# A constant operand for the clock warm-up, an own buffer for the second row tile, and its load on ScalarE's queue

## The chip, the cores and the metric

The kernel runs on one core of one Trainium2 chip. The metric is the device time of one execution in microseconds (us), lower is better. "The trace" is the hardware profile of one execution, and its times count from the start of the span. The span is about 1.7 us shorter than the device time (193.2 against 194.91 us in the profiled run of before).

## The reference

A LayerNorm without gain feeds two branches, and both are added to the input: sliding-window attention (32 heads of 16, 8 keys at distance 2) and a gated GELU feed-forward network.

```python
# x: [1, 2048, 512] bf16; wqkv [512, 1536], wo [512, 512]; w_gate, w_up [512, 1376], w_down [1376, 512]
xn = _layernorm(x, axis=-1)                       # eps 1e-5
return x + _A_ref(xn, A_wqkv, A_wo) + _B_ref(xn, B_w_gate, B_w_up, B_w_down)
# _B_ref: (gelu(xn @ w_gate) * (xn @ w_up)) @ w_down
```

## The kernel before

The program builds a graph of tasks with priorities, and a scheduler in the source lays them out on the five engines. The 2048 rows are 16 tiles of 128. Only the first tiles matter here: until tile 0 is loaded, normalized and transposed, TensorE has no real work. It runs warm-up matmuls meanwhile, which are meant to bring its clock up: in the trace of before, the step to full speed comes 5.6 us after the first of them.

```python
# warm-up: VectorE clears wsrc, TensorE multiplies it with itself
G.task("dve", "c_wsrc", 0.25, lambda e: e.memset(wsrc[:, :], 0.0), wr=[I_wsrc], prio=PC - 1)
WARM = cfg.get("WARM", ([512] * 8 + [128], [512, 128]))    # before / after the first transposes
...     # per entry: matmul(PS[...], lhsT=wsrc[:, 0:128], rhs=wsrc[:, 0:wn]), rd=[I_wsrc]

# loads: all on SyncE's queue; tile 0, tile 1, first weights (q), tile 2, weights k, tile 3, weights v, ...
t_x = G.task("sp", "ld_x%d_%d" % (p, t2), 0, mk_ld(), wr=[(it_x, t2)],
             prio=((-960, -959), (-957.8, -956.5))[p][t2], nbytes=128 * 1024)

# tile 0: VectorE (bn_stats, bn_aggr); square root on ScalarE. Tile 1: statistics on ScalarE:
#   sx1 (sum) -> negm1 (-mean) -> sxx1 (sum of squares) -> var1 (divide) -> sq1 (square root)
# then on VectorE, in place: sub (x - mean), rstd (reciprocal), norm (times rstd)

# the order that the author fixed on each engine
chain(["bnst0", "bnag0", "sub0", "rstd0", "norm0", "mean1", "sub1", "evy0_0", "rstd1", "norm1",
       "evy0_1", "bnst2", ...])                                                        # VectorE
chain(["sx1", "sq0", "negm1", "sxx1", "var1", "sq1", "evx0_0", "evx0_1", "evq0_0", "sq2"])  # ScalarE
chain(warm_tasks[:len(WARM[0])] + ["tpx0_0"] + warm_tasks[len(WARM[0]):] +
      ["mma0_0", "tpx0_1", "mmt0_0", "mmt0_1", "mmt1_0", "tpx1_0", ...])               # TensorE

# the end of SyncE's program: before the last store, wait for all earlier transfers
if eng_name == "sp" and t is self.order["sp"][-1]:
    late = self.order["sp"][-5:]
    for (s, tot) in self.dma_totals:
        if not any(q.sem is s for q in late):
            e.wait_ge(s, tot)
...
for q in self.order["sp"][-5:]:      # after the last store
    e.wait_ge(q.sem, q.val)
```

Names used below: the *first transposes* are tpx0_0 (tile 0), the *first projection* is mma0_0 (eight matmuls of 128 columns on tile 0), and *tile 1's projections* begin with mmt0_1.

## Time and profile before

| | |
|---|---|
| device time, median of 3 | 194.56 us (194.54 to 194.84) |
| the profiled execution | 194.91 us |
| TensorE busy | 97% of the span |
| first warm-up matmul, first transposes, first projection | 1.51, 5.04, 6.23 us |
| clock step to full speed | 7.1 us |

The clock is read from the matmuls too: before the step, the warm-up matmuls of 512 columns start 0.427 us apart and matmuls of 128 columns 0.107; after it, those of 128 columns start 0.056 us apart. "Cold" and "slow" below mean the first pace, "warm" the second.

The prediction below shows the engines, the chain and the timeline. Here are the lines that it only tells. First two lines of the page: the span, and SyncE's transfer queue (packets, MB, share of 16 engines' span).

```profile
span 193.2 us, 3285 instructions
...
q1 hardware_dynamic: 34784, 26.83, 57.0%
```

From the timeline (start, length, engine, line, what): SyncE issues both row tiles, then the first weights.

```profile
0.80 0.88 SPq L927 DMA_DIRECT2D XIN<-in_A_x_dram  x2
...
1.72 0.43 SPq L879 DMA_DIRECT2D Wqkv<-in_A_wqkv_dram  x1
```

From the view of source line 563 (count, duration in ns, first and last start): the ten semaphore waits before the last store; by the trace's records they start about 0.06 us apart, from 190.65 to 191.20.

```profile
L563 SPq EVENT_SEMAPHORE  x10: 17/28/28, 190.6 to 191.2; - x10
```

One queue carries nearly everything, and the first issues take 0.4 to 0.5 us each. The waits run from 190.6 to 191.2 us while VectorE finishes the last block at 191.08, so they end after the data is ready.

### The profile page before, as it was taken

Reading aid. Unit: us, or ns where it says so; the run is one execution under the profiler, and the core shown is the slowest. Engines: PE = TensorE matmul, PEld = TensorE weight load, DVE = VectorE, ACT = ScalarE, POOL = GpSimd, SP = SyncE. Lnnn points to the kernel's source line nnn. Section 1 sums busy time; section 2 is a strip of 40 time slices with the busy share of each in tenths; the row PEclk is TensorE's granted clock in tenths of the full one; section 3 lists DMA queues with packets and bytes.
Section 4 is the critical chain, followed back from the end, with each engine's and each line's share of the span. In section 5 each row is a group of like instructions: output and inputs, shape, how many; then the busy total and the mean of one; then the engine's idle time right before and its main releaser. Section 6 shows DMA issues by size and latency. Waiting matters only on the chain.

```text
span 193.2 us, 3285 instructions
## 1 busy us (share of the span) xinstructions
PE 187.6 (97%) x1239; PEld 92.6 (48%) x1256; DVE 152.4 (79%) x240; ACT 106.1 (55%) x177; POOL 15.7 (8%) x31
## 2 busy tenths in 40 slices
PE   6999999999999999999999999999999999999994
PEld 2794444444444444444444444444444444444484
DVE  5699999999997975999995599998996099912132
ACT  5677565786897666703376677328276720058000
POOL 6010011110931020000000000000000000000000
PEclk9999999999999999999999999999999999999999
DMA  5999997899564014975500597420250497130121
GB/s 142 352 397 327 313 171 136 215 244 226 150 128 102 3 33 132 242 144 150 151 25 27 127 243 166 117 90 0 68 132 21 112 230 163 41 112 0 48 76 44
DMA packets 34801, 27.04 MB, mean 140 GB/s; under 512 B 11265, under 2 KB 33249, under 8 KB 34785
## 3 DMA queue, kind: packets, MB, share of 16 engines
q1 hardware_dynamic: 34784, 26.83, 57.0%
q8 instruction: 10, 0.16, 0.4%
q14 instruction: 7, 0.05, 0.1%
HBM read 19.99 MB, written 5.26 MB: 131 GB/s over the span
## 4 chain that ended last, share of the span: by engine, by line
PE 97%; issue 1%; DVE 0%; DVEq 0%
PE PS L1399 36%; PE PS L1478 20%; PE PS L1156 18%; PE PS L1474 7%; PE PS L1102 4%; PE PS L1367 4%; PE PS L1240 4%; PE PS L870 2%; PE PS L1434 2%; PE PS L1233 1%; PE PS L1044 1%; DVE OB L1498 0%; DVE wsrc L819 0%; DVE Wd L843 0%; DVEq L558 0%
## 5 line engine op out<-in xcount | busy, mean ns | idle before, releaser
L1416 ACT ACTIVATE UU<-PS 128x512 bf16<-128x512 f32 x40 | 24.1, 603 | 35.7 <-PE PS L1399 35.7
L1478 PE MATMUL PS<-Wd,HT 128*128 128x512 bf16 (+2 forms) x207 | 41.1, 345 | 0.1
L1399 PE MATMUL PS<-xnT,Wu 128*128 128x512 bf16 x155 | 39.8, 379 | 0.7 <-issue 0.5
L1399 PE MATMUL PS<-xnT,Wg 128*128 128x512 bf16 x155 | 39.2, 379 | 0.5 <-ACT OT L1379 0.2
L1210 DVE TENSOR_TENSOR UNI<-QT,KT 128x2048 bf16<-128x2048 bf16 x32 | 37.0, 1219 | 2.6 <-PE PS L1367 2.5
L1156 PE MATMUL PS<-xnT,Wqkv 128*128 128x512 bf16 x156 | 35.3, 379 | 0.2
L1421 DVE TENSOR_TENSOR HT<-GG,UU 128x512 bf16<-128x512 bf16 x40 | 16.6, 419 | 20.2 <-ACT UU L1416 20.1
L1409 ACT ACTIVATE GG<-PS 128x512 bf16<-128x512 f32 x40 | 23.7, 601 | 15.0 <-PE PS L1399 12.2
L1478 PEld LDWEIGHTS PS<-Wd,HT 128*128 128x128 bf16 x209 | 19.6, 98 | 18.6
L1399 PEld LDWEIGHTS PS<-xnT,Wu 128*128 128x128 bf16 x160 | 15.3, 98 | 19.6 <-issue 1.3
L1399 PEld LDWEIGHTS PS<-xnT,Wg 128*128 128x128 bf16 x160 | 15.5, 98 | 19.3 <-ACT OT L1379 0.4
L1156 PEld LDWEIGHTS PS<-xnT,Wqkv 128*128 128x128 bf16 x160 | 15.6, 98 | 18.6
L1347 DVE TENSOR_TENSOR BS<-BS,PT 128x2048 bf16<-128x2048 bf16 x16 | 19.6, 1223 | 0.4
L1347 DVE TENSOR_TENSOR UNI<-BS,PT 128x2048 bf16<-128x2048 bf16 x16 | 19.5, 1218 | 0.0
L1498 DVE TENSOR_TENSOR OB<-PS,XR 128x512 bf16<-128x512 f32 (+2 forms) x19 | 11.2, 604 | 10.0 <-PE PS L1478 9.9
L1474 PE MATMUL PS<-Wo,OT 128*128 128x512 bf16 (+2 forms) x76 | 16.9, 345 | 0.0
L1180 ACT ACTIVATE VT<-PS 128x512 bf16<-128x512 f32 x16 | 9.6, 597 | 4.4 <-PE PS L1156 4.4
L1379 ACT ACTIVATE OT<-PS 128x512 bf16<-128x512 f32 x16 | 8.3, 602 | 5.0 <-PE PS L1367 5.0
L944 DVE BATCH_NORM_STATS2 st<-XIN 128x6 f32<-128x512 bf16 x15 | 10.1, 686 | 0.9 <-DMA XIN<-in_A_x_dram 0.9
L1474 PEld LDWEIGHTS PS<-Wo,OT 128*128 128x128 bf16 x76 | 7.2, 98 | 7.0
L1196 POOL COPY KT<-KT 128x64 bf16<-128x64 bf16 x3 | 8.0, 2657 | 17.5 <-ACT KT L1173 16.1
L1166 ACT ACTIVATE QT<-PS 128x512 bf16<-128x512 f32 x12 | 7.2, 597 | 3.1 <-PE PS L1156 3.1
(73 smaller groups left out, 153.6 us busy)
## 6 DMA issues: line engine op xcount, KB each, us to landing
BS<-vt_scratch SPq DMA_DIRECT2D x64, 128.5 KB, 3.7
vt_scratch<-VT SPq DMA_DIRECT2D x16, 128.0 KB
XR<-in_A_x_dram SPq DMA_DIRECT2D x16, 128.0 KB, 2.3
out_dram<-OB SPq DMA_DIRECT2D x14, 128.0 KB, 1.8
Wqkv<-in_A_wqkv_dram SPq DMA_DIRECT2D x3, 512.0 KB
XIN<-in_A_x_dram SPq DMA_DIRECT2D x6, 256.0 KB, 4.5
Wg<-in_B_w_gate_dram SPq DMA_DIRECT2D x1, 1280.0 KB
Wu<-in_B_w_up_dram SPq DMA_DIRECT2D x1, 1280.0 KB
```

The costliest lines, as they stand in the source:

```text
L944: return lambda e: e.bn_stats(out=st[:, t, :], in_=XIN[:, it.slot, t2, :])
L1156: ins = e.matmul(PS[:, 512 * it.slot:512 * it.slot + HWD], lhsT=lhsT, rhs=xnT[:, itx.slot, kt, c0:c0 + HWD], start=(kt == 0), stop=(kt == 3))
L1180: return lambda e: e.activation(out=VT[:, ito.slot, 0:HWD], in_=PS[:, 512 * it.slot:512 * it.slot + HWD], func=ACTF.Identity)
L1210: return lambda e: e.tensor_tensor(out=UNI[:, it.slot, :, :], in0=bass.AP(QT, (itq.slot * 4 + g) * 512, [[NQT * 4 * 512, 128], [0, 4], [1, ...
L1347: return lambda e: e.tensor_tensor(out=dst(), in0=bass.AP(BS, it.slot * 4 * 514 + o, [[NBS * 4 * 514, 128], [514, 4], [128, 4], [1, 128]]) ...
L1399: ins = e.matmul(PS[0:M, 512 * it.slot:512 * it.slot + 512], lhsT=Wx[:, kt, j * 128:j * 128 + M], rhs=xnT[:, itx.slot, kt, :], start=(kt = ...
L1409: return lambda e: e.activation(out=GG[0:M, ito.slot, :], in_=PS[0:M, 512 * it.slot:512 * it.slot + 512], func=ACTF.Gelu_apprx_tanh)
L1416: return lambda e: e.activation(out=UU[0:M, ito.slot, :], in_=PS[0:M, 512 * it.slot:512 * it.slot + 512], func=ACTF.Identity)
L1421: return lambda e: e.tensor_tensor(out=HT[0:M, ito.slot, j, :], in0=GG[0:M, ig.slot, :], in1=UU[0:M, iu.slot, :], op=ALU.mult)
L1474: ins = e.matmul(PS[:, 512 * it.slot:512 * it.slot + CW], lhsT=OT[:, ito.slot, dq, ti * 128:(ti + 1) * 128], rhs=Wo[:, dq, c0:c1], start=( ...
L1478: ins = e.matmul(PS[:, 512 * it.slot:512 * it.slot + CW], lhsT=HT[:, ith.slot, j, ti * 128:(ti + 1) * 128], rhs=Wd[:, j, c0:c1], start=Fal ...
L1498: return lambda e: e.tensor_tensor(out=OB[:, ito.slot, 0:CW], in0=PS[:, 512 * it.slot:512 * it.slot + CW], in1=XR[:, itx.slot, c0:c1], op= ...
```

## The change

Its intent is to shorten the start and the end, the only places where TensorE isn't working. Warm-up matmuls read a constant that GpSimd writes at 0.36 us, before the other engines start at about 0.8, so TensorE can begin at once. Tile 1's load is issued by ScalarE at the same moment as tile 0's on SyncE. Tile 1 is centred into its own buffer XS, so VectorE need not wait until ScalarE has read the tile; and the division by 512 moves into the square root's scale, so var1 goes. The waits at the end move three stores ahead.

```diff
-            if eng_name == "sp" and t is self.order["sp"][-1]:
-                late = self.order["sp"][-5:]
+            if eng_name == "sp" and t is self.order["sp"][-4]:
+                late = self.order["sp"][-7:]
...
-            for q in self.order["sp"][-5:]:
+            for q in self.order["sp"][-7:]:
...
-        wsrc = sb("wsrc", [128, 512], BF)
+        one_l = nc.const_aps.tensor(1.0, [128, 128], BF)
+        one_r = nc.const_aps.tensor(1.0, [128, 512], BF)
...
+        XS = sb("XS", [128, 512], BF)
...
-        WARM = cfg.get("WARM", ([512] * 8 + [128], [512, 128]))
+        WARM = cfg.get("WARM", ([512] * 9 + [128], [512, 128, 128, 128, 128]))
...
+                    t_x.on_act = p == 0 and t2 == 1
...
-                            ("var1", 0.2, dict(out=mv[:, 1, 1:2], in_=sums[:, 2:3], ...
+                        return lambda e: e.activation(out=sq[:, 1:2], in_=sums[:, 2:3], func=ACTF.Sqrt,
+                                                      scale=1.0 / D, bias=eps[:, 0:1])
...
+                if t == 1:
+                            out=XS[:, :], in0=XIN[:, it.slot, 1, :], scalar1=mv[:, 1, 0:1], scalar2=None,
...             # norm1 reads XS instead of XIN; the rest renames, drops an unused option, and follows from this
```

More of the change, by code (lines that the diff above doesn't have):

```diff
@@ L674, in bass_parallel_sum__sliding_local_dilated__glu_gated_geglu__prompt_kernel @@
     NXIN = cfg.get("NXIN", 4)
-    NSUBA = cfg.get("NSUBA", 0)
     NSQA = cfg.get("NSQA", 4)
@@ L800, in bass_parallel_sum__sliding_local_dilated__glu_gated_geglu__prompt_kernel @@
         I_zpad = Item("zpad")
-        I_wsrc = Item("wsrc")
         I_onef = Item("onef")
@@ L809, in bass_parallel_sum__sliding_local_dilated__glu_gated_geglu__prompt_kernel @@
         I_sums = Item("sums")
+        I_xs = Item("XS")
         I_junk = Item("junk")
@@ L818, in bass_parallel_sum__sliding_local_dilated__glu_gated_geglu__prompt_kernel @@
         PC2 = cfg.get("PC2", 8)
-        G.task("dve", "c_wsrc", 0.25, lambda e: e.memset(wsrc[:, :], 0.0), wr=[I_wsrc], prio=PC - 1)
         G.task("pool", "c_ones", 0.2, lambda e: e.memset(cf[:, :], 1.0), wr=[I_cf], prio=PC)
@@ L869, in mk_w @@
             def mk_w(it=it_warm, wn=wn):
-                return lambda e: e.matmul(PS[:, 512 * it.slot:512 * it.slot + wn], lhsT=wsrc[:, 0:128],
-                                          rhs=wsrc[:, 0:wn], start=True, stop=True)
-            t_w = G.task("pe", "warm%d" % i, d_mm(wn), mk_w(), rd=[I_wsrc], wr=[it_warm], prio=-400, mode="f")
+                return lambda e: e.matmul(PS[:, 512 * it.slot:512 * it.slot + wn], lhsT=one_l,
+                                          rhs=one_r[:, 0:wn], start=True, stop=True)
+            t_w = G.task("pe", "warm%d" % i, d_mm(wn), mk_w(), wr=[it_warm], prio=-400, mode="f")
             t_w.urgent = True
@@ L951, in bass_parallel_sum__sliding_local_dilated__glu_gated_geglu__prompt_kernel @@
                             ("sxx1", 0.55, dict(out=XR[:, 0, :], func=ACTF.Square, bias=sums[:, 1:2],
-                                                accum_out=sums[:, 2:3]), [(I_sums, 1)], [I_junk, (I_sums, 2)]),
-                            ("var1", 0.2, dict(out=mv[:, 1, 1:2], in_=sums[:, 2:3], func=ACTF.Identity,
-                                               scale=1.0 / D), [(I_sums, 2)], [(I_mv, "v1")])):
+                                                accum_out=sums[:, 2:3]), [(I_sums, 1)], [I_junk, (I_sums, 2)])):
                         def mk_a(kw=kw, it=it_x):
@@ L978, in bass_parallel_sum__sliding_local_dilated__glu_gated_geglu__prompt_kernel @@
                 if t < NSQA:
-                    t_of["sq%d" % t] = G.task("act", "sq%d" % t, 0.15, mk_sa(), rd=[(I_mv, "v1" if t == 1 else t), I_eps],
+                    t_of["sq%d" % t] = G.task("act", "sq%d" % t, 0.15, mk_sa(), rd=[(I_sums, 2) if t == 1 else (I_mv, t), I_eps],
                                               wr=[(I_sq, t)], prio=pr - 100, table="sqrt")
@@ L1003, in mk_sub @@
                         scalar2=None, op0=ALU.subtract)
-                if t < NSUBA:
-                    def mk_sub(t=t, t2=t2, it=it_x):
-                        return lambda e: e.activation(
-                            out=XIN[:, it.slot, t2, :], in_=XIN[:, it.slot, t2, :], func=ACTF.Identity,
-                            scale=-1.0, bias=mv[:, t, 0:1])
-                t_of["sub%d" % t] = G.task("act" if t < NSUBA else "dve", "sub%d" % t,
-                                           0.6 if t < NSUBA else 0.27, mk_sub(), rd=[(it_x, t2), (I_mv, t)],
-                                           wr=[(it_x, t2)], prio=tp0(t) + 2)
+                if t == 1:
+                    def mk_sub(it=it_x):
+                        return lambda e: e.tensor_scalar(
+                            out=XS[:, :], in0=XIN[:, it.slot, 1, :], scalar1=mv[:, 1, 0:1], scalar2=None,
+                            op0=ALU.subtract)
+                t_of["sub%d" % t] = G.task("dve", "sub%d" % t, 0.27, mk_sub(), rd=[(it_x, t2), (I_mv, t)],
+                                           wr=[I_xs if t == 1 else (it_x, t2)], prio=tp0(t) + 2)
                 def mk_nm(t=t, t2=t2, it=it_x):
-                    if t < NSUBA:
-                        return lambda e: e.tensor_scalar(
-                            out=XIN[:, it.slot, t2, :], in0=XIN[:, it.slot, t2, :], scalar1=rstd[:, t:t + 1],
-                            scalar2=-1.0, op0=ALU.mult, op1=ALU.mult)
                     return lambda e: e.tensor_scalar(
-                        out=XIN[:, it.slot, t2, :], in0=XIN[:, it.slot, t2, :], scalar1=rstd[:, t:t + 1],
+                        out=XIN[:, it.slot, t2, :], in0=XS[:, :] if t == 1 else XIN[:, it.slot, t2, :], scalar1=rstd[:, t:t + 1],
                         scalar2=None, op0=ALU.mult)
-                t_of["norm%d" % t] = G.task("dve", "norm%d" % t, 0.27, mk_nm(), rd=[(it_x, t2), (I_rstd, t)],
+                t_of["norm%d" % t] = G.task("dve", "norm%d" % t, 0.27, mk_nm(), rd=[I_xs if t == 1 else (it_x, t2), (I_rstd, t)],
                                             wr=[(it_x, t2)], prio=tp0(t) + 4)
@@ L1134, in bass_parallel_sum__sliding_local_dilated__glu_gated_geglu__prompt_kernel @@
                                wr=[(it_qt, ("t", t)) if which == 0 else (KTI[0], ("t", t))], prio=-100 + t)
-                chain(["sx1", "sq0", "negm1", "sxx1", "var1", "sq1", "evx0_0", "evx0_1", "evq0_0", "sq2"])
+                chain(["sx1", "sq0", "negm1", "sxx1", "sq1", "evx0_0", "evx0_1", "evq0_0", "sq2"])
                 chain(["evx1_0", "sq3"])
```

## The prediction

> **What bounds the kernel now.** I read the busy shares and the chain that ended last first, then that chain in order of time, then the timeline of the first 10 us.
>
> ```profile
> PE 187.6 (97%) x1239; PEld 92.6 (48%) x1256; DVE 152.4 (79%) x240; ACT 106.1 (55%) x177; POOL 15.7 (8%) x31
> ...
> PE 97%; issue 1%; DVE 0%; DVEq 0%
> ```
>
> The first line is the busy time of each engine, the second the chain that ended last by engine. TensorE is both. Ordered by time (start, length, what), the chain reads so at its two ends:
>
> ```profile
> 1.18 0.28 DVE wsrc L819
> ...
> 1.51 3.70 PE PS L870 x9
> 5.21 0.44 PE PS L1044 x4
> 5.65 0.53 PE PS L870 x2
> ...
> 6.23 1.02 PE PS L1102 x8
> 7.25 0.22 PE PS L1044 x4
> 7.48 0.45 PE PS L1102 x8
> ...
> 7.96 1.96 PE PS L1102 x32
> ...
> 190.78 0.29 DVE OB L1498
> ```
>
> L870 is the warm-up, L1044 the transposes of the normalized rows, L1102 the first projections. From 6.23 us (first projection) TensorE runs nearly without a gap to 190.69 us; the remaining "issue" entries are 0.03 to 0.16 us each. The change neither removes nor shortens any of that work. Only 0 to 8 us and the 2.5 us after TensorE's end are open to it. The reader should also see the clock: four transposes take 0.44 us at 5.21 but 0.22 us at 7.25, and eight projections 1.02 us at 6.23 but 0.45 us at 7.48. The clock record of the trace has the step to full speed at 7.1 us, 5.6 us after the first warm-up matmul. At half speed the first projections therefore cost about 0.45 us too much.
>
> What prepares the first two row tiles, from the timeline:
>
> ```profile
> 2.91 0.69 DVE L944 BATCH_NORM_STATS2 st<-XIN 128x6 f32<-128x512 bf16 x1 [0.91 <-DMA XIN<-in_A_x_dram]
> 3.49 0.63 ACT L956 ACTIVATE XR<-XIN 128x512 bf16<-128x512 bf16 x1 [1.20 <-DMA XIN<-in_A_x_dram]
> 4.12 0.28 ACT L976 ACTIVATE sq<-mv,eps 128x1 bf16<-128x1 bf16 x1
> 5.04 0.61 PE L1044 MATMUL PS<-ident,XIN 128*128 128x128 bf16 x4
> 5.37 0.21 ACT L956 ACTIVATE mv<-sums 128x1 bf16<-128x1 f32 x1
> 5.37 0.35 DVE L1001 TENSOR_SCALAR XIN<-XIN,mv 128x512 bf16<-128x512 bf16 x1 [0.32 <-ACT XR L956]
> 5.61 0.30 ACT L976 ACTIVATE sq<-mv,eps 128x1 bf16<-128x1 bf16 x1
> 5.69 0.29 DVE L1056 COPY xnT<-PS 128x256 bf16<-128x256 bf16 x1
> 5.81 0.36 ACT L1064 ACTIVATE xnT<-PS 128x256 bf16<-128x256 bf16 x1
> 5.94 0.16 DVE L994 RECIPROCAL rstd<-sq 128x1 f32<-128x1 bf16 x1
> 6.14 0.35 DVE L1018 TENSOR_SCALAR XIN<-XIN,rstd 128x512 bf16<-128x512 bf16 x1
> ```
>
> VectorE does tile 0, ScalarE the statistics of tile 1, which come 0.58 us later because SyncE issues the two loads one after the other. ScalarE's eviction at 5.81 releases the first projection at 6.23. The fourth line (first transposes) waits for tile 0 on VectorE, which in turn waited for the square root of tile 0 (4.12), which sat behind tile 1's sum on ScalarE.
>
> [...] Here one issue takes 0.40 to 0.51 us on SyncE. [...]
>
> **The change part by part.**
> 1. *Constant warm-up.* The memset of wsrc goes. Its wait goes too: other engines start 0.80 to 0.91 us after the span's start, so TensorE should start at about 0.85 instead of 1.51, 0.65 us earlier. Ten matmuls (9x512+128 columns) at 0.427 us per 512 are 3.95 us and end at about 4.8 us (before 5.0). This doesn't shorten the path by itself: the transposes wait for tile 0 anyway. What it may bring is the clock's step. If the step follows the first matmul by a fixed time, it comes at 6.5 instead of 7.1[...]. Gain between 0 and 0.45 us, which is all that the cold projections waste.
> 2. *Longer second warm-up* (1024 columns instead of 640): cold this is 0.85 us instead of 0.53. After transposes from about 4.96 to 5.39 it ends near 6.25, so in a cold run the first projection can't start before 6.25, as now; in a warm run it takes half as long and is not felt.
> 3. *Load on ScalarE's queue.* Tile 1 should land about 0.35 us earlier, at some 3.1 us. [...] 256 KB at once instead of 128, so tile 0 may land 0.1 to 0.2 us later (its landing record now ends at 2.89). Earlier tile 1 lets the square root of tile 0 run at once: it started 4.12, while its input was ready at 3.82. The two nearly cancel: I expect the transposes at 4.9 to 5.0 instead of 5.04, gain 0.05 to 0.1. The SyncE loads behind move up by one issue, 0.46 us; the first weights landed at 5.91 us by the landing record, close to 6.23, so this keeps them out of the way. ScalarE's table load (1.28 us) slips by 0.4 us and ends near 2.5, still before tile 1.
> 4. *Own buffer XS, and var1 dropped.* The centring of tile 1 waited 0.32 us for ScalarE's read, and var1 held ScalarE about 0.24 us. Both are gone. But the next VectorE step is the copy at 5.69, which waits for the transposes, and the reciprocal and scaling of tile 1 stand behind it in VectorE's order. So tile 1 is done at about 6.4 instead of 6.49. ScalarE's first eviction moves from 5.81 to about 5.73, when the transposes are through. Gain under 0.1 us, already counted in 3.
> 5. *Waits before the last store.* Nine of ten of the semaphore instructions move three stores ahead. The last store's data is ready at 191.07 and it was issued at 191.27; it should go at about 191.12. Gain 0.15 us. Two more waits after it find their stores landed: nothing.
> 6. *Order in the middle.* The scheduler swaps some groups of four matmuls and some VectorE work; the counts stay. The current order has no stalls to win, so this is between -0.1 and +0.2 us.
>
> Sum: 0.15 (tail) + 0.1 (preparation) + 0.1 to 0.2 (clock[...]). The three timed runs, 194.54 to 194.84, lie below the profiled one (194.91), so in the median run the clock may already step before the first projections, and then its gain is small. I take 0.35 off 194.56.
>
> **The rivals.** *No gain at all:* the two loads delay each other, the first projection waits for the longer warm-up, the clock's step stays where it is, and only the tail's 0.15 us are left: 194.4. For it: the first projection had three conditions within 0.3 us of each other (weights 5.91, eviction 6.17, warm-up 6.18), so taking away one brings the next. *The full clock gain:* the step before 6 us in nearly all runs, first projections at 6.15 all warm, about 0.5 us at the start plus the tail: 193.9. For it: TensorE's earlier start and the unbroken warm-up. Against: the timed runs seem to have part of it already. *A new stall in the middle* from the changed order, or loads that now arrive in another order: 194.8. Against it: the gate weights landed at 15.9 us and are needed at 17.4, and the chain of before shows no wait of TensorE on a load.
>
> **Range and chances.** All outcomes lie between the full gain and a small loss, 193.75 to 194.65 with run-to-run noise of 0.3. Two per cent would be 3.9 us, more than all that the start and the tail have to give (6.23 us before the first projection, most of it load latency and the normalization chain), so "same" is almost certain. I predict 194.2 us.
>
> **What would show it.** TensorE's first matmul near 0.85 (part 1); the first transposes at 4.9 to 5.0 and tile 1's sum at about 3.1 (part 3); no gap before tile 1's centring (part 4) but the scaling of tile 1 still after 6 us; the first projection at 6.1 to 6.3 and whether its eight matmuls take 1.0 or 0.45 us (the clock); the last store within 0.1 us of VectorE's end (part 5); TensorE's stretch from first projection to its end between 183.9 and 184.6 us. I would be wrong if tile 0 landed much later than 3.1, if the middle showed new waits of TensorE, or if the first projection came well before 6 us.

Marked cuts are statements that no trace of this case shows: on what the clock's step follows, on how the two queues are served, and on where the semaphore instructions at the end come from. 0.15 (tail), 0.1 (preparation) and 0.1 to 0.2 (clock) came to 0.35 to 0.45 us, of which 0.35 was taken. The clock's term is my estimate, a part of the 0.45 us that the cold projections lose; the reasons for part 1's lower end of 0 (the step might not move at all) and for taking an average are among the cuts.

## The result

| | median | lowest to highest | runs |
|---|---|---|---|
| before | 194.57 us | 194.54 to 194.84 | 4 |
| changed | 194.58 us | 194.40 to 194.72 | 4 |

The ratio is 0.9997, with a 95% interval of 0.998 to 1.0014: no difference. A ratio here is the mean time of one kernel's fast runs over that of the other's of the same rounds, so it isn't quite the ratio of the medians. The prediction was 194.2 in a range of 193.75 to 194.65.

The profile of the changed kernel isn't the old one, though. From its page: the span, the two queues, and the chain by engine.

```profile
span 192.9 us, 3287 instructions
...
q10 hardware_dynamic: 144, 0.13, 0.2%
...
PE 95%; DMA 1%; issue 1%; ACT 1%; DVE 1%; DVEq 0%
```

The chain now holds a transfer and ScalarE, which it didn't before, and more of VectorE. In order of time (start, length, what):

```profile
0.80 2.88 DMA XIN<-in_A_x_dram
...
3.70 0.70 DVE st L945
...
4.65 0.30 ACT sq L978
...
5.07 0.82 ACT XR L955 x2
...
5.92 0.30 ACT sq L976
6.21 0.28 ACT xnT L1061
...
6.54 0.62 PE PS L1099 x8
7.16 0.22 PE PS L1041 x4
...
7.86 1.96 PE PS L1099 x32
```

Compare this with the chain of before. There it ran through the warm-up matmuls on TensorE from 1.51 us; here it starts with tile 0's load, which takes until 3.68 us. The first projection is at 6.54 instead of 6.23, that is *later*. But it is warm: from its start to that of tile 1's projections it takes 1.32 us instead of 1.73, so these begin at 7.86 instead of 7.96. The timeline of the same stretch:

```profile
0.79 0.40 ACTq L927 DMA_DIRECT2D XIN<-in_A_x_dram  x1
...
0.80 0.40 SPq L927 DMA_DIRECT2D XIN<-in_A_x_dram  x1
...
0.83 4.01 PE L870 MATMUL PS<-const-bfloat16-1.0 128*128 128x512 bf16 x10 [0.83 <-PEq L1549]
...
3.53 0.63 ACT L955 ACTIVATE XR<-XIN 128x512 bf16<-128x512 bf16 x1 [0.81 <-DMA XIN<-in_A_x_dram]
3.70 0.69 DVE L945 BATCH_NORM_STATS2 st<-XIN 128x6 f32<-128x512 bf16 x1 [1.99 <-DMA XIN<-in_A_x_dram]
...
5.59 0.40 PE L1041 MATMUL PS<-ident,XIN 128*128 128x128 bf16 x4 [0.74 <-DVE mv L958]
5.63 0.35 DVE L1008 TENSOR_SCALAR XS<-XIN,mv 128x512 bf16<-128x512 bf16 x1
...
6.45 0.35 DVE L1015 TENSOR_SCALAR XIN<-XS,rstd 128x512 bf16<-128x512 bf16 x1
```

TensorE starts at 0.83 as planned, and the two loads are issued within 0.01 us of each other. But tile 1's sum starts at 3.53 (before: 3.49), not earlier, and tile 0's statistics at 3.70 (before: 2.91), 0.79 us later. The two lines with "DMA" in their brackets show that both engines waited for their loads. At the other end, source line 563 reads:

```profile
L563 SPq EVENT_SEMAPHORE  x9: 17/28/28, 186.6 to 187.5; - x9
```

The waits are out of the way: the last store is issued at 191.00, 0.03 us after VectorE's end (before: 0.19).

### The profile page after: what moved, and what is told of

Read it like the earlier page. It is cut to its first block, busy times and chain, and to the rows that moved or that the text cites. A ratio compares the mean times of both kernels' runs of the same rounds, so it can differ in the third digit from the quotient of the medians.

```text
span 192.9 us, 3287 instructions
## 1 busy us (share of the span) xinstructions
PE 187.4 (97%) x1244; PEld 92.4 (48%) x1260; DVE 151.6 (79%) x239; ACT 105.9 (55%) x176; POOL 15.6 (8%) x31
## 4 chain that ended last, share of the span: by engine, by line
PE 95%; DMA 1%; issue 1%; ACT 1%; DVE 1%; DVEq 0%
PE PS L1396 36%; PE PS L1475 20%; PE PS L1153 18%; PE PS L1471 7%; PE PS L1099 4%; PE PS L1364 4%; PE PS L1237 4%; PE PS L1431 2%; DMA XIN<-in_A_x_dram 1%; PE PS L1230 1%; ACT XR L955 0%; DVE st L945 0%; PE PS L1041 0%; ACT sq L976 0%; ACT sq L978 0%
```

## The experiments

One number orders all of them. In 12 of the 14 profiles, the stretch from the start of tile 1's projections to the start of TensorE's last matmul is 182.50 us, whatever the kernel and however the scheduler shuffled the middle. (It is longer in d1, whose clock was slow for longer, and in c2, which waited for a later load.) From that last start to the end of the span it is 2.74 us in the three profiles with the old waits at the end, and 2.57 to 2.58 in the eleven with the moved ones. So the time is decided by when tile 1's projections begin, plus the tail. All kernels gave correct results; each experiment has five or six executions (d1 four). c1, u2, c2 and a3 ran on one chip, the other eight on another. "Mean" is the mean of a kernel's runs less the mean of the runs of before on the same chip (for the first result, 194.63; then 194.79 to 194.81, and 194.68). The start times are from each kernel's one profile.

| kernel | median | mean, less before | ratio (95%) | tile 0, tile 1, first weights landed | first projection | tile 1's projections |
|---|---|---|---|---|---|---|
| before | 194.57 to 194.66 | 0 | 1 | 2.89, 3.47, 5.91 | 6.23 (cold) | 7.96 |
| changed, first result | 194.58 | -0.06 | 0.9997 (0.998 to 1.0014) | 3.68, 3.51, 5.31 | 6.54 | 7.86 |
| a2_after | 194.77 | -0.04 | 0.9996 (0.9978 to 1.0013) | 3.64, 3.46, 5.27 | 6.52 | 7.84 |
| a3_after | 194.36 | -0.21 | 0.9993 (0.998 to 1.0007) | 3.38, 3.53, 5.37 | 6.23 | 7.55 |
| o1_load_act | 195.00 | +0.17 | 1.0006 (0.999 to 1.0022) | 3.31, 3.48, 5.33 | 6.40 | 7.75 |
| o2_warm | 194.53 | -0.29 | 0.9983 (0.9968 to 0.9998) | 3.03, 3.45, 6.12 | 6.25 | 7.56 |
| o3_tail | 194.42 | -0.31 | 0.9977 (0.996 to 0.9994) | 2.95, 3.43, 5.97 | 6.19 (cold) | 8.10 |
| u1_load_sp | 194.48 | -0.26 | 0.9985 (0.9965 to 1.0004) | 3.02, 3.39, 6.97 | 7.11 | 8.41 |
| u2_load_sp | 194.36 | -0.36 | 0.9984 (0.9971 to 0.9996) | 2.91, 3.29, 6.00 | 6.13 | 7.44 |
| c1_warm_tail | 194.38 | -0.33 | 0.9985 (0.9973 to 0.9998) | 2.99, 3.44, 5.71 | 6.20 | 7.52 |
| t1_tiny_act | 194.47 | -0.28 | 0.9983 (0.9965 to 1.0) | 3.08, 3.38, 6.41 | 6.54 | 7.85 |
| b1_wq_act | 194.67 | -0.09 | 0.9992 (0.9976 to 1.0009) | 2.96, 3.41, 6.26 | 6.39 | 7.70 |
| d1_delay_act | 198.45 | +3.5 | 1.0176 (1.0146 to 1.0205) | 2.96, 6.02, 5.99 | 8.85 (cold) | 10.98 |
| c2_split_wq | 195.27 | +0.49 | 1.0028 (1.0015 to 1.004) | 2.92, 3.35, 4.97 and 5.77 | 6.08 | 7.39 |

Theory A: the parts do gain, but two loads that start together hold tile 0 back, and that eats the gain. Rival B: there never was a gain, and tile 0's landing only scatters.

### u1_load_sp and u2_load_sp: the load goes back to SyncE

```diff
-                    t_x.on_act = p == 0 and t2 == 1
```

> The changed kernel with one part undone: tile 1's load goes back to SyncE's queue, second after tile 0's. Theory A (two loads issued together hold tile 0 back, and this eats the other gains): tile 0's load lands at about 2.9 us again instead of 3.68, the first transposes start at 4.9 to 5.1 instead of 5.59, the first projection at 6.1 to 6.25 instead of 6.54, and the time is 194.1 to 194.3, about 0.3 to 0.4 us under the changed kernel. Rival B (tile 0's landing just scatters from run to run, or something else holds the first projection): no difference from the changed kernel beyond 0.1 us, about 194.55.

> Second sample of the changed kernel with tile 1's load on SyncE; its first profile had a first weight load that landed at 6.97 us and held the first projection to 7.11. If that was a rare event: weights at 5.9 to 6.2, first projection at 6.1 to 6.3, mean 194.3 to 194.45. If the weights often land late when issued at 1.72 us: mean 194.5 again, with single runs over 194.9.

Tile 0 landed at 3.02 and 2.91 us again, and the first transposes came at 4.97 and 4.87 instead of 5.32 to 5.59. So the cause of tile 0's delay is in the one line that was undone. From the timeline of u2_load_sp:

```profile
2.94 0.69 DVE L944 BATCH_NORM_STATS2 st<-XIN 128x6 f32<-128x512 bf16 x1 [1.22 <-DMA XIN<-in_A_x_dram]
```

But u1's profile brought a new wait. From its view of TensorE's waits (total us, times, longest):

```profile
PE PS L1098 <- DMA Wqkv<-in_A_wqkv_dram: 1.1, 1, 1.1
```

The first weights landed at 6.97 us and the first projection waited for them until 7.11. In the other kernels with both tiles on SyncE they landed at 5.71 to 6.41. In the changed kernel they land at 5.27 to 5.37, since SyncE issues them one issue earlier (at 1.25 to 1.26 instead of 1.72 us), and are never felt. So the queue change has a good side that I had not put a number on.

u2 waits for the weights too, though its view doesn't say so. The eviction by ScalarE and the first projection:

```profile
5.40 0.36 ACT L1060 ACTIVATE xnT<-PS 128x256 bf16<-128x256 bf16 x1
...
6.13 0.61 PE L1098 MATMUL PS<-xnT,Wqkv 128*128 128x128 bf16 x8 [0.40 <-DVE XIN L1014]
```

The bracket names a step of VectorE that the first projection doesn't read. The eviction, which it does read, had ended at 5.76; the weights landed at 6.00. The first projection starts 0.14 us after the weights' landing in u1, u2, o2, t1 and b1, and 0.05 to 0.06 us after the eviction's end in before, o1, o3, c1 and all three profiles of the changed kernel. So with the row tiles both on SyncE and the shorter statistics of tile 1 (u1, u2, t1 and b1; c2 splits the weights), it is the first weights that set the first projection, and undoing the queue change trades one wait for another.

Beside the unaltered changed kernel, u2's mean was 0.15 us lower and the medians were equal (194.36); on the other chip, u1's mean was 0.21 lower. Both point the same way, but neither difference is clear of the scatter of the runs. u1's landing of tile 0 is what theory A expected, but its mean, 194.55, is what rival B did. Its profiled run, 195.21, is the slowest of its six by 0.46 us, so weights as late as 6.97 weren't the rule.

### a2_after and a3_after: the changed kernel again

No edit: the changed kernel as it is, on the chip of u1, o1, o2 and o3 in the one case and beside u2 in the other.

> The changed kernel unaltered, once more, on the same chip as the three other runs of this call. Theory: tile 0's load lands again at 3.3 to 3.7 us, first transposes at 5.3 to 5.6, first projection at 6.4 to 6.6, warm; time 194.5 to 194.6, within 0.15 us of the mean of before or up to 0.25 under it. If the late landing was chance: tile 0 at 3.0 and a first projection at 6.2.

> The changed kernel unaltered beside these three. Expected: tile 0 lands at 3.3 to 3.7 us, first projection at 6.4 to 6.6 warm, mean 194.65 to 194.8, that is 0.2 to 0.4 us above the version with the load on SyncE; the spread of the times is small, since neither the clock's step nor the weights limit it. If it is within 0.1 us of u2, the queue change costs nothing on balance.

Tile 0 landed at 3.64 and 3.38 us, the first transposes came at 5.55 and 5.32, and the first projection at 6.52 and 6.23. So the late landing of the first result repeats, in three profiles of three, and rival B's "only scatter" falls for the landing: the latest landing of tile 0 in a kernel whose tile 1 stays on SyncE is 3.08. Its size does scatter, by 0.3 us, and the packet records show with what. Where SyncE's queue carried its first 1 KB packet before ScalarE's (at 1.85 against 1.93 us in a3, 1.82 against 1.95 in o1 below), tile 0 landed at 3.38 and 3.31; where ScalarE's was first (1.82 against 1.95 in the first result, 1.82 against 2.08 in a2), at 3.68 and 3.64. In all four the packets of the two tiles are mixed: SyncE's 128th packet ended at 2.76 to 2.95, against 2.50 in before.

In the timed runs the delay is far less clear: the means are -0.04 and -0.21 against before. a3's mean, 194.48, is below the 194.65 to 194.8 that was expected, a miss.

### o1_load_act: this part alone

```diff
+                    t_x.on_act = p == 0 and t2 == 1     # in the kernel before
```

> The kernel before with only this part: tile 1's load issued by ScalarE. Theory A: tile 0's load lands at 3.5 to 3.8 us instead of 2.89, the transposes start near 5.6, the first projection at 6.6 to 6.8, and the time is 0.2 to 0.4 us above before, 194.8 to 195.0. Rival B: tile 0's landing within 0.2 us of before and no change of the time beyond 0.1 us.

Tile 0 landed at 3.31 us. From the timeline:

```profile
3.33 0.70 DVE L945 BATCH_NORM_STATS2 st<-XIN 128x6 f32<-128x512 bf16 x1 [1.34 <-DMA XIN<-in_A_x_dram]
```

The delay is 0.42 us here, less than the 0.49 to 0.79 in the changed kernel, and the first projection came at 6.40, not after 6.6. The median was 0.34 us above that of before, the mean only 0.17, and the interval includes 1. The direction is that of theory A. The landing and the first projection are earlier than it expected (3.5 to 3.8 and 6.6 to 6.8); the mean, 194.97, is where it expected it.

### t1_tiny_act: a second queue, without the bytes

```diff
+        t_d = G.task("sp", "ld_tiny", 0, lambda e: e.dma_start(XR[0:16, 1, :], x2[1024:1040, :]), ...)
+        t_d.on_act = True          # tile 1 stays on SyncE
```

> The changed kernel with tile 1's load back on SyncE, and in its place on ScalarE's queue a load of 16 KB [...] that nothing reads. If the bytes of tile 1 hold tile 0 back: tile 0 lands by 3.05 us as in the kernels with both loads on SyncE (2.89 to 3.03). If a second queue that starts at the same moment is what delays it, whatever its size: tile 0 lands at 3.3 to 3.7 us as with the whole tile.

```profile
3.10 0.69 DVE L947 BATCH_NORM_STATS2 st<-XIN 128x6 f32<-128x512 bf16 x1 [1.39 <-DMA XIN<-in_A_x_dram]
```

Tile 0 landed at 3.08 us, 0.03 above the limit set for it, but 0.23 or more below every landing beside the whole tile. A second queue that starts at the same moment with 16 KB is nearly harmless, so it is what tile 1 carries (128 KB in 128 packets) that holds tile 0 back. Bytes and packets were reduced together; which of the two counts isn't shown. The time of t1 doesn't tell what tile 0 costs, because the first projection waited for the weights:

```profile
6.54 0.61 PE L1101 MATMUL PS<-xnT,Wqkv 128*128 128x128 bf16 x8 [0.71 <-DMA Wqkv<-in_A_wqkv_dram]
```

### d1_delay_act: ScalarE's load 0.6 us later

```diff
                     assert not t.waits
+                    q = next(x for x in self.tasks if x.name == "c_id")     # a GpSimd step
+                    e.wait_ge(q.sem, q.val)
```

> The changed kernel with ScalarE's load held back by a wait on a GpSimd semaphore, so that it is issued near 1.4 us, 0.6 us after tile 0's load. If sharing in time is the cause: tile 0 lands at 2.9 to 3.1 us, tile 1 at 3.6 to 3.9, first transposes near 5.0 and the first projection at 6.2 to 6.4 (tile 1's late statistics now hold ScalarE); time 0 to 0.2 us under the changed kernel. If the second queue itself is the cause: tile 0 still at 3.3 or later and no gain.

Half of it came out: issued at 1.40 us, the load left tile 0 alone (2.96). But it now came behind the first weights, which SyncE had issued at 1.25. From the chain:

```profile
1.40 4.62 DMA XIN<-in_A_x_dram
```

Tile 1's 128 KB were counted as landed at 6.02 us, together with the weights' 512 KB (5.99). By the packet records, its packets ran from 3.6 to 5.2 us between the weights' packets. Tile 0 was held up with it, because its square root stands behind tile 1's sum on ScalarE, which began at 6.04. So the first transposes slipped to 7.59 and TensorE paused for over 2.6 us; in this run the clock's step came only at 13.4 us, and the kernel lost 3.5 us. Both theories had missed this: in this run the small load, issued after a large one on the other queue, landed over 2.5 us later than where it comes second on the same queue (3.29 to 3.47).

### o2_warm and o3_tail: two parts alone

```diff
-rd=[I_wsrc], lhsT=wsrc[:, 0:128], rhs=wsrc[:, 0:wn]      # o2: with the c_wsrc memset removed
+lhsT=one_l, rhs=one_r[:, 0:wn]                           # and the new WARM lengths
```

> The kernel before with only the constant warm-up in its new lengths. If the clock's step follows TensorE's first matmul: the first matmul at 0.83 us, the step by 6.5 us or earlier, the eight first projections in 0.45 to 0.6 us instead of 1.02, time 194.2 to 194.4. If the step falls independently of the start: [...] the mean time is within 0.15 us of before, with a longer second warm-up that can even cost 0.05 us.

The first matmul was at 0.84, the step at about 3.8 us (by the spacing of the matmuls; this trace has no clock record), and the first projection at 6.25, warm. The six runs lie between 194.40 and 194.64, so neither branch came out whole: the projections are warm as the first has it, but the time is not under 194.4, and the mean gained more than the second allows. The kernel before, on the same chip, has two groups: seven runs from 194.38 to 194.66 and five from 195.08 to 195.27. The warm-up removes the upper group; against the lower one, it gains nothing. The step came 2.9 to 6.0 us after the first matmul over the 13 profiles other than d1's (5.6 in before, 6.0 in o3_tail, 5.0 in o1_load_act, 3.8, 5.0 and 3.7 in the three of the changed kernel). With the first matmul at 1.51 that reaches past the first projection: the step was at 7.1 in before and 7.5 in o3. With 0.83 to 0.84 it was at 5.9 or earlier in all ten, before the first projection. So the step doesn't follow the first matmul by a fixed time; what sets it, these traces don't show. That the upper group of before is the late steps is what the scatter of the step suggests. One run was both timed and profiled and supports it: o3's 194.98, the slowest of its six, is the one with the step at 7.5. The timed runs of before have no traces to show it.

> The kernel before with only the semaphore waits moved from the last store to the fourth from the end. If those waits were on the path: the last store is issued within 0.05 us of VectorE's end instead of 0.2 us after it, and the time falls by 0.15 to 0.2 us, to 194.4. If the store's landing or the closing steps hide it: no change.

The edit is the first two hunks of the diff. The last store was issued at 191.25, 0.03 us after VectorE's end instead of 0.19. The mean fell by 0.31 us, of which about 0.17 can be the waits (the tail of 2.57 instead of 2.74 us); its runs also had the late clock group only once in six (194.98), which I take for chance.

### c1_warm_tail: the two parts that gain, without XS

The kernel before with the edits of o2 and o3 together.

> The kernel before with two parts of the change only: the constant warm-up and the moved waits; loads, in-place centring and var1 as before. If the parts add up from the runs with one part each (means 0.27 and 0.15 to 0.3 us under before): mean 194.3 to 194.4. If own buffer and dropped var1 are worth something, the changed kernel with its load back on SyncE (u2) is faster than this one by 0.1 us or more; if not, the two agree within 0.1 us.

Mean 194.35 against 194.32 for u2, which has XS and no var1 besides: in the time, these two parts are worth nothing that can be seen. In the traces they are. Tile 0's square root and ScalarE's eviction are 1.69 to 1.70 us apart in the five profiles with var1, and 1.45 to 1.47 in six of the nine without (1.53 to 1.57 in the other three, whose transposes ran with the slow clock). In c1 the eviction starts later than u2's 5.40:

```profile
5.78 0.36 ACT L1063 ACTIVATE xnT<-PS 128x256 bf16<-128x256 bf16 x1
```

But u2 then waits for weights that landed at 6.00 (c1: 5.71), so c1 and u2 don't tell what the earlier eviction is worth. Dropping var1 alone was not run. A kernel with XS alone couldn't be built, because the on-chip memory is full: with XS added to before, the build stops at OB, which needs 4096 bytes per partition and finds 3072. The kilobyte per partition of XS is that of wsrc, so the constant warm-up pays for it.

### b1_wq_act and c2_split_wq: attempts at a faster version

```diff
+            t_w.on_act = nm == "q"       # b1: from u1, with the GpSimd wait of d1 before the issue
```

> A version meant to beat both: the changed kernel with both row tiles on SyncE's queue, and the first weights (512 KB) on ScalarE's queue behind the same wait, issued near 1.4 us instead of 1.72. Expected: tile 0 lands by 3.1, the weights at 5.4 to 5.8 instead of 5.9 to 7.0, first projection at 6.1 to 6.2 warm, time 194.1 to 194.3. If the weights' packets hold the tiles back as tile 1's do: tile 1 lands after 3.6 and the time is 194.5 or more.

The weights were issued at 1.40 instead of 1.72 but landed at 6.26, not earlier than on SyncE, and SyncE had issued tile 2 by 2.16, long before they landed. A miss.

```diff
-    Wqkv[:, :, 0:512] in one load        # c2: from u1, told in words
+    Wqkv[:, :, 0:256], then Wqkv[:, :, 256:512]; the first eight matmuls wait for the first half only
```

> As u2, with the first weight load split into two halves of 256 KB, of which the first projection's first eight matmuls need only one. If the weights' landing is what now limits the first projection: first half lands near 5.2 us, first projection at 6.05 to 6.15, the spread of the times shrinks and the mean is 194.2 to 194.3. If the halves (512-byte rows) load more slowly or the second half comes too late: a wait between the first and second eight projections and no gain.

The first half landed at 4.97 and the first projection came at 6.08, as hoped, right behind a second warm-up that ran mostly with the slow clock (5.33 to 6.08). But the weights k behind landed at 9.08 instead of about 7.8, and TensorE waited for them:

```profile
PE PS L1101 <- DMA Wqkv<-in_A_wqkv_dram: 0.7, 1, 0.7
```

That is a loss of 0.5 us against before, and of 0.85 against u2. The halves differ from the one load in their rows of 512 bytes and in one more issue; which of the two goes with the slower stream isn't shown.

## Why the prediction held, and where a step of it failed

1. *What bounds the kernel.* Right. The middle stayed at 182.50 us; only start and tail moved.
2. *Constant warm-up* (start at 0.85, gain 0 to 0.45). Right: 0.83 to 0.84, and 0.29 us in the mean of o2, nothing against the lower group of before, which I take for the runs that had stepped in time. That the timed runs of before have part of the gain already was the right reason to discount it.
3. *Longer second warm-up.* Right in both cases. Warm, it is not felt: in u2 it ends at 5.73, and the first projection waits for the weights. With the slow clock, in d1, it ran from 7.99 to 8.85, the 0.85 us predicted, and the first projection started as it ended, 0.23 us after the eviction.
4. *Load on ScalarE's queue.* **This step failed.** It said that tile 1 lands "some 3.1 us" and that tile 0 "may land 0.1 to 0.2 us later", and that the two "nearly cancel" with a gain of 0.05 to 0.1. Tile 1 landed at 3.46 to 3.53, not earlier at all (on SyncE: 3.29 to 3.47), and tile 0 0.4 to 0.8 us later than in before (3.31 to 3.68; with tile 1 on SyncE 2.89 to 3.08). The transposes came at 5.30 to 5.59 instead of 4.9 to 5.0. The prediction had named this as a sign of being wrong, "if tile 0 landed much later than 3.1". I had taken the time between the two landings for issue time. It was time that the two transfers take together: 256 KB are there by 3.3 to 3.7 us, in either arrangement, and the second queue only decided whether tile 0 was done first. The side effect on the first weights was right in sign, and in all but c1 larger than the 0.46 us of one issue: 5.3 instead of 5.7 to 7.0.
5. *Own buffer, no var1.* Half right. The gap before the centring is gone, and the time shows nothing (c1 and u2 differ by 0.03 us). But the reason given, that the eviction waits for the transposes anyway, holds only where these ran with the slow clock, as in u1. In the changed kernel the eviction follows tile 0's square root by 1.47 us instead of 1.69, and the first projection follows the eviction, so this part shortened the path by about 0.22 us, and the late tile 0 used that up.
6. *Tail.* Right: 0.15 predicted, 0.16 measured between VectorE's end and the store, and 0.17 up to the end of the span.
7. *Order in the middle.* Right, and smaller than allowed: 182.50 us before and after.

The sum, 0.35 us off, measured -0.06, -0.04 and -0.21 in three samples. So the time, 194.58, was covered by the width of the range, 0.07 us from its upper end, and not by the sum. Between the profiles of before and of the first result, two terms missed in opposite directions: the first projection came 0.31 us later (0.1 earlier was predicted), and the stretch from there to tile 1's projections was 0.41 us shorter by the clock (0.1 to 0.2 was predicted). With the 0.17 us of the tail this makes the 0.27 us by which the two spans differ. That the clock covered the delay here is luck: the profiled run of before had a late step, and seven of its twelve runs on the chip of o2 are as fast as the runs with the new warm-up.

The warm-up and the tail gave 0.33 us together (c1). In the profiles the shared load takes part of it back (tile 1's projections at 7.55 to 7.86 against 7.52 in c1). How much of the time it costs isn't settled: the changed kernel's mean is 0.15, 0.21 and 0.13 us above those of u2, u1 and c1 on the same chip, within the scatter, and in u1 and u2 the weights come in its place. The rival "no gain at all" named this mechanism (the two loads delay each other) and, with 194.4, was nearer the time than the main line. Open are: how often the weights land as late as in u1, whether c1 or u2 beats the changed kernel in the timed runs (the profiles say 7.52 for c1, and 7.44 and 8.41 for u2 and u1, which are one kernel, against 7.55 to 7.86; the times do not settle it), and why tile 1 in d1 was counted as landed only with the weights.

Both c1 and u2 beat the kernel before by about 0.15%, with intervals that exclude 1; the interval of u1 includes it.

## What to carry to other kernels

Before moving a load to a second queue, look at the packets: here the packets of the two loads were mixed: the second one didn't arrive sooner (3.46 to 3.53 us, on one queue 3.29 to 3.47), and the more urgent one arrived later (3.31 to 3.68 against 2.89 to 3.08). Order loads by who waits for them first; here a single queue kept that order. Then look at what comes next: once tile 0 was early again, the first weights were the last to arrive. And where a wait names an engine that the instruction doesn't read from, compare the landing times: a fixed distance over several runs (0.14 us here) tells which wait it was. Where a kernel is bound by one engine, find the point from which its stream runs without a gap; here every change before it was worth what it moved that point, to 0.01 us in 12 profiles.
